# A fused attention and mixer kernel: chunk 3's first channel product in seven half-size products, the last stores in smaller pieces, and all jobs in another order

## The chip, the core and the metric

The kernel runs on one NeuronCore of a Trainium2 chip. The core has TensorE (PE, matmuls; PEld is its loading of weights), VectorE (DVE), ScalarE (ACT), GpSimd (POOL) and SyncE (SP). Each engine works through its own list of instructions in order and waits on semaphores for the others. PE writes only to the eight banks of PSUM, which VectorE and ScalarE read; DMAs move data between HBM and on-chip memory and are issued by SP, ACT and POOL. The metric is the time of one execution on the device in microseconds.

## The reference, cut to what matters

```python
q_p, k_p = phi(q * scale), phi(k * scale)     # exp features, 128 of them; batch 8, heads 8, seq 576, dim 64
kv  = einsum('bhsm,bhsd->bhmd', k_p, v);  z = sum(k_p, axis=2)
x   = einsum('bhsm,bhmd->bhsd', q_p, kv) / (einsum('bhsm,bhm->bhs', q_p, z) + 1e-6)
x   = x.transpose(0, 2, 1, 3).reshape(8, 576, 512)
h   = relu(x^T @ w_tok1) @ w_tok2             # token mixing: 576 -> 256 -> 576
u   = x + h^T
out = u + relu(u @ w_ch1) @ w_ch2             # channel mixing: 512 -> 1536 -> 512
```

Inputs and output are float32; the matmuls run on float16 operands.

## The kernel before

The work is cut into nine chunks of 512 rows for the channel mixing: chunk b (0 to 7) is the first 512 rows of batch b, and chunk 8 holds the 64 remaining rows of all eight batches. For each batch there are three stages.

*Attention* (`attention`): `kp` and `qp` are the feature matmuls (L702, L714) and `kt`, `qt` those of the 64 last rows (L594, L664); ScalarE takes their exponentials from the banks (L557); VectorE finds maxima (L735) and reciprocals; `vs_` scales v by them (L751, through the helper at L338); `kv` and `num` are the remaining products (L758, L791); `scale` divides the result out of the bank into x, on VectorE in one instruction (L809) or on ScalarE in five (L807).

*Token mixing* (`token_mix`): two products (L826, L839), an add that makes u (L842), and a DMA transpose on SP that turns u into uT (`ut_dma`, L847). For batches 2 to 7 q and k are cast by GpSimd's DMAs into a scratch in HBM and come back through DMA transposes on SP into qT and kT (`back`, L423); each of the two has three buffers.

*Channel mixing* (`channel_mix`): the second product, r3 @ w_ch2, uses seven half-size products instead of eight (`channel_out_fast`, L984, 256 columns each) in chunks 1 to 8; VectorE or GpSimd makes the half-sums S (L928), and VectorE reads the banks and adds (`read`, L964). The first product, uT @ w_ch1, has two forms. The plain one takes twelve blocks of four matmuls of 512 columns (L1167; L1173 and L1175 for chunk 0's first two) and a relu for each block. The fast one (`channel_in_fast`, chunks from `FAST_IN` on) takes three groups of seven products of four matmuls of 256 columns (L1096). Per group ScalarE copies three partial banks out (`keep`, L1115), VectorE joins them with later banks (`join`, L1120), and relus follow. Its operands are four differences of uT per chunk (L1067) and, once for all chunks, eight differences of w_ch1 (`weight_sums`, L1052), which occupy one buffer each of qT and kT from then on.

The order of the work is written out. Every piece of work is a job with a number, given in the order in which the functions add them. `ORDER` lists all job numbers in the order in which they are put into the engines' lists; a negative number is a filler matmul on zeros (`warm`, L1241). `SLOT` gives the buffer number of each tile, `MOVED` the engine of a job where it isn't the usual one. The planner only checks this order; it chooses nothing. A dependence becomes a semaphore wait, so a job early in `ORDER` can still wait. Jobs marked `port=True` on VectorE and GpSimd also wait for each other in turn (`turns`), so that they do not run at the same time.

The stores of chunks 2 to 7 are two per chunk (L1026), those of chunk 8 twelve (L1019).

Job numbers that the prediction's steps use (new numbers where they differ): 0 is the identity; 7, 17, 12 and 10 are loads (k's tail, w_tok1, the two halves of q); 1219 is chunk 7's kT transpose, 960 chunk 5's uT transpose; 1132, 1134 and 1130 are the last of chunk 6's second token products, 1023, 1025, 1027 and 1030 four output products of chunk 5, 859 and 860 stores of chunk 4, 1396 a tail transpose, 1138 chunk 6's uT transpose, 1175 chunk 6's first channel product.

Of the kernel before, what the change touches and what calls it, by code (L numbers as in the profile page):

```python
# [208 lines left out]
def kernel(  # L209
# [12 lines left out]
    nc = tc.nc  # L222
# [3 lines left out]
    DM = H * D  # L226
# [8 lines left out]
    NCB = DC // P  # L235
    NU = H // 2
    R = SM // 2
    RT = ST // 2
    RA = R + RT
    NPE = 2  # L240
    FAST_IN = 4
    SPLIT = ()
    HALVES = ()
    RW = S * 4 // P
    c_scale = float(1.0 / math.sqrt(math.sqrt(D)))

    pool = ctx.enter_context(tc.tile_pool(name="sb", bufs=1))
# [1027 lines left out]
```

## Time and profile before

| | us |
|---|---|
| runs | 272.42, 274.98, 272.96 |
| median | 272.96 |
| span of the profiled execution (its total is not given beside it) | 271.2 |
| TensorE busy | 262.6 |
| VectorE busy | 225.1 |
| ScalarE busy | 167.4 |
| GpSimd busy | 149.9 |

The span runs from the first to the last instruction of one profiled execution; the times of the runs also hold what lies around it. An engine's busy time is the union of its instructions. The granted TensorE clock is 0.997 of full speed over the span. A row of the chain of waits has a start, a length and what ran; a row of the waits has the waiting engine and line, what it waited for, the total, how often, and the longest; a row of the timeline has a start, a length, engine, line, operation, out<-in, shapes and count, and in brackets the idle time before it.

### The profile page before, as it was taken

Reading aid. Unit: us, or ns where it says so; the run is one execution under the profiler, and the core shown is the slowest. Engines: PE = TensorE matmul, PEld = TensorE weight load, DVE = VectorE, ACT = ScalarE, POOL = GpSimd, SP = SyncE. Lnnn points to the kernel's source line nnn. Section 1 sums busy time; section 2 is a strip of 40 time slices with the busy share of each in tenths; the row PEclk is TensorE's granted clock in tenths of the full one; section 3 lists DMA queues with packets and bytes.
Section 4 is the critical chain, followed back from the end, with each engine's and each line's share of the span. In section 5 each row is a group of like instructions: output and inputs, shape, how many; then the busy total and the mean of one; then the engine's idle time right before and its main releaser. Section 6 shows DMA issues by size and latency. Waiting matters only on the chain.

```text
span 271.2 us, 6792 instructions
## 1 busy us (share of the span) xinstructions
PE 262.6 (97%) x2683; PEld 183.9 (68%) x2683; DVE 225.1 (83%) x483; ACT 167.4 (62%) x395; POOL 149.9 (55%) x155
## 2 busy tenths in 40 slices
PE   8899999999999999999999999999999999999992
PEld 4457455444557655775468687886698688888882
DVE  3888879759879779988888989989987986899882
ACT  2999942179683639637965989777768342482400
POOL 8895393066882694662898893692551025404041
PEclk9999999999999999999999999999999999999998
DMA  7999999998999999999846999701160182030026
GB/s 195 191 208 210 191 211 183 192 217 148 196 234 172 251 219 150 163 236 192 163 91 103 214 130 221 187 2 77 39 139 2 21 155 81 2 155 2 19 87 209
DMA packets 81297, 39.72 MB, mean 146 GB/s; under 512 B 63984, under 2 KB 77040, under 8 KB 81072
## 3 DMA queue, kind: packets, MB, share of 16 engines
q0 software_dynamic: 31744, 17.74, 44.1%
q1 hardware_dynamic: 46928, 15.37, 28.5%
q10 hardware_dynamic: 2592, 6.16, 6.0%
q8 instruction: 21, 0.34, 0.5%
q14 instruction: 12, 0.10, 0.1%
HBM read 35.95 MB, written 16.52 MB: 193 GB/s over the span
## 4 chain that ended last, share of the span: by engine, by line
PE 91%; ACT 3%; DMA 3%; DVE 1%; issue 0%
PE bank L984 27%; PE bank L1096 16%; PE bank L1167 15%; PE bank L826 5%; PE bank L839 5%; PE bank L1201 4%; PE bank L791 3%; PE bank L702 3%; PE bank L758 3%; DMA kT<-k 3%; PE bank L714 2%; PE bank L1241 1%; ACT kp L557 1%; PE bank L513 1%; PE bank L793 1%; PE bank L819 1%
## 5 line engine op out<-in xcount | busy, mean ns | idle before, releaser
L338 POOL TENSOR_TENSOR vs<-v,vs 128x512 f16<-128x512 f16 x31 | 32.7, 1060 | 24.4 <-DVE vs L739 9.6
L1167 PE MATMUL bank<-uT,wc 128*128 128x512 f16 x184 | 44.1, 379 | 0.0
L557 ACT ACTIVATE kp<-bank 128x512 f16<-128x512 f32 x64 | 34.9, 617 | 14.5 <-PE bank L702 14.5
L333 ACT ACTIVATE r<-bank 128x512 f16<-128x512 f32 (+1 forms) x52 | 30.6, 607 | 19.4 <-PE bank L1167 8.4
L984 PEld LDWEIGHTS <-r 128*128 128x128 f16 x384 | 36.6, 98 | 6.5 <-issue 1.9
L735 DVE TENSOR_REDUCE km<-kp 128x8 f16<-128x1024 f16 x32 | 38.2, 1203 | 2.3 <-ACT kp L557 2.3
L557 ACT ACTIVATE qp<-bank 128x512 f16<-128x512 f32 x64 | 35.6, 620 | 3.4 <-PE bank L714 3.4
L338 POOL TENSOR_TENSOR r<-r 128x768 f16<-128x768 f16 x9 | 14.7, 1641 | 33.7 <-DVE S L338 20.5
L984 PEld LDWEIGHTS <-S 128*128 128x128 f16 x288 | 27.7, 98 | 4.0 <-DVE S L338 0.3
L1167 PEld LDWEIGHTS <-wc 128*128 128x128 f16 x184 | 16.4, 97 | 16.7 <-issue 1.0
L984 PE MATMUL bank<-T,r 128*128 128x256 f16 x192 | 23.6, 273 | 0.0
L984 PE MATMUL bank<-T,S 128*128 128x256 f16 x192 | 23.6, 273 | 0.0
L984 PE MATMUL bank<-wc,r 128*128 128x256 f16 x192 | 23.3, 273 | 0.0
L807 ACT ACTIVATE x<-bank,rc 128x64 f16<-128x64 f32 x90 | 20.6, 353 | 4.3 <-DVE rc L798 2.9
L338 POOL TENSOR_TENSOR S<-r,S 128x768 f16<-128x768 f16 x10 | 16.3, 1644 | 11.8 <-DVE r L338 9.3
L809 DVE TENSOR_TENSOR x<-bank,rc 128x320 f16<-128x320 f32 x46 | 21.5, 482 | 0.8
L335 DVE TENSOR_SCALAR r<-bank 128x512 f16<-128x512 f32 (+1 forms) x29 | 19.0, 664 | 3.6 <-PE bank L1167 2.4
L964 DVE TENSOR_TENSOR o<-u,bank 128x512 f32<-128x512 f16 x28 | 18.9, 676 | 3.5 <-PE bank L984 3.4
L1096 PE MATMUL bank<-uT,wc 128*128 128x256 f16 x156 | 21.1, 273 | 0.0
L842 DVE TENSOR_TENSOR u<-x,bank 128x512 f16<-128x512 f16 x28 | 17.9, 682 | 2.2 <-PE bank L839 2.0
L1096 PEld LDWEIGHTS <-wc 128*128 128x128 f16 x180 | 17.1, 98 | 2.7
L791 PEld LDWEIGHTS <-qp 128*128 128x128 f16 x256 | 13.6, 98 | 4.2 <-issue 0.4
(157 smaller groups left out, 576.0 us busy)
## 6 DMA issues: line engine op xcount, KB each, us to landing
out_dram<-o ACTq DMA_DIRECT2D x9, 512.0 KB, 3.1
q<-in_q_dram POOLq DMA_DIRECT2D x6, 576.0 KB, 7.9
wc<-in_moe_w_ch_dram POOLq DMA_DIRECT2D x4, 768.0 KB, 10.6
k<-in_k_dram POOLq DMA_DIRECT2D x6, 512.0 KB, 8.1
v<-in_v_dram POOLq DMA_DIRECT2D x6, 512.0 KB, 8.0
out_dram<-o SPq DMA_DIRECT2D x5, 512.0 KB, 3.4
r<-in_q_dram POOLq DMA_DIRECT2D x4, 288.0 KB, 7.2
v<-in_v_dram POOLq DMA_DIRECT2D x4, 256.0 KB, 8.9
```

The source lines that it names most:

```text
L333: nc.scalar.activation(out=out, in_=in_, func=AF.Relu)
L335: nc.vector.tensor_relu(out=out, in_=in_)
L338: (nc.gpsimd if eng == "POOL" else nc.vector).tensor_tensor(**kw)
L557: nc.scalar.activation(out=out, in_=in_, func=AF.Exp, bias=0.0, scale=1.0)
L735: nc.vector.reduce_max(out=t_km[place("km", (b, hp))], in_=src_, axis=AX.X)
L791: nc.tensor.matmul(ps[:, k, j * 65 : (j + 1) * 65], st, s[:, i, 0 : D + 1], start=True, stop=True)
L807: nc.scalar.activation(out=to[:, j], in_=ps[:, j], func=AF.Copy, scale=rc[:, j : j + 1])
L809: nc.vector.tensor_tensor(out=to, in0=ps, in1=rc.unsqueeze(2).broadcast_to((P, NJ + 1, D)), op=ALU.mult)
L964: nc.vector.tensor_tensor(out=o, in0=a, in1=ps, op=ALU.add)
L984: nc.tensor.matmul(ps[:, j * DH : (j + 1) * DH], a[:, cb, j * P : (j + 1) * P], w[:, cb, :], start=(bank_of(b, j0) not in held and j == j0 ...
L1096: nc.tensor.matmul(ps[:, n, :], w(a)[:, (2 * m + n) * P : (2 * m + n + 1) * P], x_[:, a], start=(what in ("P1", "P2", "P5") and n == 0 and ...
L1167: nc.tensor.matmul(ps, wc1[:, db, cb * P : (cb + 1) * P], moving(db), start=(db == 0), stop=(db == ND - 1))
```

## The change

`FAST_IN` goes from 4 to 3, so that chunk 3's first channel product takes the fast form as chunks 4 to 8 do, and `weight_sums` is placed before chunk 3. The tail's store of the block "22" is cut into two pieces and leaves from SP and ACT by default; chunk 7's second store is cut into its right and its left half. The job numbers shift accordingly (1500 jobs for 1469), and `ORDER`, `SLOT` and `MOVED` are new throughout, with 15 fillers instead of 16. `MOVED` puts, among others, 24 evictions of x on ScalarE instead of 18, 20 products `vs_` on GpSimd instead of 31, 30 half-sums S on GpSimd instead of 24, 20 differences of uT there instead of 11, and 10 of the copies `keep` on VectorE instead of none.

```diff
 ORDER = [
-    2, 5, 0, 6, 3, 1, 4, 16, 14, 18, 15, 7, 38, 12, -1, -2, -3, -4, -5, 39, 40, -6, 45, 9, 8, 47, 46, 10, 112, 41,
...
+    7, 2, 16, 5, 17, 12, 10, 0, 9, 1, 38, -8, -7, 39, 40, 14, 49, 50, 18, 45, 6, 3, 47, 48, 46, 112, 69, 114, 113,
+    70, 72, 71, 4, 41, 43, 21, 11, 8, 13, 29, 28, 19, 22, 30, 20, 73, 42, 118, 44, 129, 54, 78, 95, 130, 79, 80, 96,
...
+    1117, 1084, 818, 834, 1118, 1219, 684, 960, 961, 1223, 1233, 1077, 1225, 1224, 1235, 1079, 1234, 1078, 832, 819,
...
+    1272, 1271, 1132, 1133, 1134, 1130, 1135, 1131, 1023, 1236, 1253, 1287, 1025, 1255, 1254, 1276, 1264, 1288,
+    1238, 1289, 1237, 1277, 859, 860, 1396, 1138, 1017, 1016, 1020, 1024, 1290, 1027, 1261, 1247, 1278, 1281, 1244,
+    1265, 1291, 1026, 1292, 1293, 1028, 1030, 1245, 1294, 1248, 1246, 1282, 1283, 1266, 1279, 1295, 1296, 1297,
+    1249, 1280, 1175, 1298, 1144, 1143, 1262, 1031, 1299, 1178, 1300, 1139, 1140, 1263, 1022, 1018, 1142, 1159,
...
+    1465, 1466, 1469, 1388, 1463, 1467, 1455, 1475, 1471, 1472, 1476, 1477, 1470, 1391, 1453, 1457, 1486, 1487,
+    1490, 1491, 1473, 1474, 1482, 1483, 1478, 1479, 1496, 1497, 1492, 1493, 1480, 1481, 1494, 1495, 1488, 1489,
+    1484, 1485, 1499, 1498,
 ]
...
-    FAST_IN = 4
+    FAST_IN = 3
...
-            for i, js, cols, need in ((0, (0, 2), left, "11"), (1, (0, 2), right, "22"), (0, (0, 1), right, "12"), (0, (1, 2), right, "12"),
-                                      (1, (0, 1), left, "21"), (1, (1, 2), left, "21")):
+            for i, js, cols, need in ((0, (0, 2), left, "11"), (1, (0, 1), right, "22"), (1, (1, 2), right, "22"), (0, (0, 1), right, "12"),
+                                      (0, (1, 2), right, "12"), (1, (0, 1), left, "21"), (1, (1, 2), left, "21")):
                 for h in range(2):
-                    eng = engine("POOL" if need == "22" else "ACT" if h else "SP")
+                    eng = engine("ACT" if h else "SP")
...
-        for i, need in ((0, ["11", "12"]), (1, ["21", "22"])):
+        pieces = [(0, slice(0, DM), ["11", "12"])]
+        if c < B - 1:
+            pieces.append((1, slice(0, DM), ["21", "22"]))
+        else:
+            pieces += [(1, slice(DH, DM), ["22"]), (1, slice(0, DH), ["21"])]
+        for i, cols, need in pieces:
             eng = engine("SP")
-            def store(i=i, eng=eng):
-                (nc.scalar if eng == "ACT" else nc.sync).dma_start(out=out[c, 0:SM, :].rearrange("(p j) d -> p j d", j=NJ)[:, 2 * i : 2 * i + 2, :], in_=o_of(i))
+            def store(i=i, cols=cols, eng=eng):
+                (nc.scalar if eng == "ACT" else nc.sync).dma_start(
+                    out=out[c, 0:SM, :].rearrange("(p j) d -> p j d", j=NJ)[:, 2 * i : 2 * i + 2, cols], in_=o_of(i)[:, :, cols])
             dma(eng, key + 0.9 + 0.1 * i, 1.3, store, deps=[outs[x, 0] for x in need], give=[o_tag(i)], cost=0.4)
```

In the new `ORDER`, the numbers on SP's queue around the places that the prediction names are, in this order: 784 (chunk 4's uT), 1219, 684 (a store of chunk 3), 960, and later 859, 860, 1396, 1138. Before it was 1110 for chunk 6's uT, 932 for chunk 5's, and chunk 7's kT was 1191, behind 932. Between chunk 6's second token products and its first channel product PE has, in the new list, 1023, three `qp`, 1025, a `kv`, a `num`, 1027, five `num`, a `kv`, 1030 and a `num`.

More of the change, by code (lines that the diff above doesn't have):

```diff
@@ L22 @@
 ORDER = [
[72 rows of a table removed]
[73 rows of a table added]
 ]
 SLOT = (
-    "0100234050600701103402521706330411560210401223120233033711614250603121274011353162700434056100673712"
-    "5604012137412011364072310230050171020343162253332400316147113252670150234273510456726122307162037060"
-    "2101403611743101500672132341016022340210153710060304721221311256200137405034166217310045360007231160"
-    "0514120035104163352201116013521130226023322300247231215031762225103506445703673205406111010711533212"
-    "1607431356207050146101037210023042621132416151237110114621370004437262522017230341625300127411073652"
@@ L102 @@
-    "7052306430302500224170306211134520211603340201152261201003530146001042170476635123150410171020302341"
-    "0713007123003024072311231042171200363451106172341125001274320451011005735620031131500035146134011672"
-    "3350140201372623547000632172523461301322524114020721020456357476031036732361103062040230607211045210"
-    "713221066004351206702201016412202076415102"
+    "0010203450670010102315407026132510700231246110175023271340351163304522012017423030455673071061570423"
+    "1643520117216004523311271460110123002761502413361072101356711420222150234003750614567371004020301743"
@@ new lines @@
+    "1120036105427650322110042230176051013110012170635325311406230271412040173551347266025313741001602013"
+    "7425110074335217420100112213122514701023041507131013642174233424067705425361570600302416011500720311"
+    "1611024173300203610422030721213046121032110331423673305010627120124103671431455121301027502230220331"
+    "0003365610213400710500224336711024030761103400120470633200111274060502763074150226047533012625701103"
+    "1021231314267415326014235210614332140511106314701530231067514111107504333162550012016202200151677567"
@@ L106 @@
+    "1034103022000216235174320362500123417120021135421137143507712502060074312630125423350630421075136012"
+    "0134021030232613475013200017103625600123167400"
 )
 MOVED = {
-    44: "ACT", 48: "ACT", 53: "ACT", 61: "ACT", 64: "ACT", 67: "ACT", 68: "ACT", 108: "ACT", 120: "DVE",
-    122: "ACT", 128: "ACT", 139: "ACT", 147: "DVE", 149: "DVE", 153: "DVE", 157: "ACT", 159: "DVE", 167: "DVE",
-    171: "DVE", 173: "DVE", 175: "ACT", 179: "DVE", 185: "DVE", 191: "ACT", 197: "ACT", 207: "ACT", 208: "DVE",
@@ L111 @@
-    229: "ACT", 246: "ACT", 304: "DVE", 314: "DVE", 316: "DVE", 320: "DVE", 322: "DVE", 328: "POOL", 334: "POOL",
-    350: "ACT", 402: "ACT", 413: "DVE", 436: "ACT", 439: "DVE", 452: "DVE", 454: "DVE", 456: "DVE", 458: "DVE",
-    468: "DVE", 470: "DVE", 478: "POOL", 482: "POOL", 527: "DVE", 550: "ACT", 561: "DVE", 564: "ACT", 602: "DVE",
-    604: "DVE", 606: "DVE", 624: "DVE", 627: "POOL", 628: "POOL", 629: "POOL", 630: "POOL", 631: "POOL",
-    632: "POOL", 647: "ACT", 648: "ACT", 711: "DVE", 717: "ACT", 734: "ACT", 739: "DVE", 750: "POOL", 751: "POOL",
@@ L116 @@
-    752: "POOL", 753: "POOL", 756: "POOL", 757: "POOL", 758: "POOL", 760: "POOL", 809: "POOL", 810: "POOL",
-    812: "POOL", 814: "POOL", 816: "POOL", 831: "ACT", 861: "DVE", 878: "DVE", 898: "ACT", 901: "ACT",
-    936: "POOL", 937: "POOL", 938: "POOL", 952: "DVE", 953: "ACT", 954: "ACT", 970: "ACT", 987: "POOL",
-    988: "POOL", 992: "POOL", 1009: "ACT", 1039: "DVE", 1045: "ACT", 1059: "ACT", 1076: "ACT", 1093: "ACT",
-    1099: "DVE", 1101: "DVE", 1113: "POOL", 1145: "ACT", 1146: "ACT", 1162: "ACT", 1164: "POOL", 1168: "POOL",
@@ L121 @@
-    1185: "ACT", 1186: "ACT", 1235: "ACT", 1238: "ACT", 1252: "ACT", 1255: "ACT", 1289: "POOL", 1292: "POOL",
-    1324: "ACT", 1338: "DVE", 1342: "POOL", 1348: "POOL", 1363: "ACT", 1364: "ACT", 1371: "POOL", 1372: "POOL",
-    1404: "ACT", 1419: "ACT", 1420: "ACT", 1424: "POOL", 1428: "POOL",
+    42: "DVE", 44: "ACT", 46: "ACT", 50: "DVE", 52: "ACT", 58: "ACT", 59: "ACT", 61: "ACT", 67: "ACT", 86: "DVE",
+    103: "DVE", 108: "ACT", 120: "DVE", 137: "DVE", 139: "ACT", 147: "DVE", 149: "DVE", 157: "ACT", 161: "ACT",
@@ new lines @@
+    164: "DVE", 173: "DVE", 183: "ACT", 185: "DVE", 187: "DVE", 191: "ACT", 202: "ACT", 206: "ACT", 208: "DVE",
+    227: "DVE", 266: "ACT", 278: "DVE", 289: "DVE", 304: "DVE", 314: "DVE", 318: "DVE", 326: "DVE", 328: "POOL",
+    330: "POOL", 332: "POOL", 334: "POOL", 350: "ACT", 377: "DVE", 394: "DVE", 396: "DVE", 402: "ACT", 411: "DVE",
+    413: "DVE", 419: "ACT", 428: "DVE", 433: "ACT", 439: "DVE", 456: "DVE", 458: "DVE", 466: "DVE", 476: "POOL",
+    477: "POOL", 478: "POOL", 481: "POOL", 482: "POOL", 527: "DVE", 533: "ACT", 542: "DVE", 547: "ACT", 559: "DVE",
@@ new lines @@
+    561: "DVE", 584: "ACT", 587: "DVE", 603: "POOL", 605: "POOL", 606: "POOL", 609: "POOL", 610: "POOL",
+    611: "POOL", 612: "POOL", 660: "ACT", 662: "POOL", 666: "POOL", 713: "DVE", 716: "ACT", 736: "ACT", 750: "ACT",
+    767: "ACT", 785: "POOL", 786: "POOL", 787: "POOL", 788: "POOL", 792: "DVE", 803: "ACT", 804: "ACT", 813: "DVE",
+    840: "POOL", 842: "POOL", 844: "POOL", 889: "DVE", 892: "ACT", 909: "ACT", 926: "ACT", 940: "DVE", 943: "ACT",
+    946: "ACT", 963: "POOL", 965: "POOL", 966: "POOL", 981: "ACT", 982: "ACT", 997: "ACT", 998: "ACT", 1013: "ACT",
@@ new lines @@
+    1014: "ACT", 1017: "POOL", 1019: "POOL", 1020: "POOL", 1022: "POOL", 1037: "ACT", 1067: "DVE", 1073: "ACT",
+    1087: "ACT", 1104: "ACT", 1107: "ACT", 1139: "POOL", 1141: "POOL", 1142: "POOL", 1146: "DVE", 1165: "DVE",
+    1174: "ACT", 1181: "DVE", 1189: "ACT", 1190: "ACT", 1192: "POOL", 1194: "POOL", 1196: "POOL", 1198: "POOL",
+    1213: "ACT", 1249: "ACT", 1260: "DVE", 1280: "ACT", 1300: "ACT", 1317: "POOL", 1319: "POOL", 1320: "POOL",
+    1324: "DVE", 1334: "DVE", 1335: "ACT", 1336: "ACT", 1345: "DVE", 1352: "ACT", 1367: "ACT", 1368: "ACT",
@@ L124 @@
+    1370: "POOL", 1372: "POOL", 1373: "POOL", 1374: "POOL", 1376: "POOL", 1391: "ACT", 1398: "POOL", 1399: "POOL",
+    1400: "POOL", 1405: "DVE", 1416: "ACT", 1426: "DVE", 1431: "DVE", 1432: "ACT", 1433: "ACT", 1440: "DVE",
+    1453: "POOL", 1455: "POOL", 1457: "POOL", 1486: "ACT", 1487: "SP", 1488: "POOL", 1489: "POOL", 1492: "ACT",
+    1493: "SP", 1494: "ACT", 1495: "SP",
 }
```

134 rows, old and new, of the table ORDER are left out of this document.

## Prediction

> **What bounds the kernel now.** I read the page first, then the waits of TensorE alone, then the chain of waits in order of time, and last the stretches.
>
> ```profile
> span 271.2 us, 6792 instructions
> PE 262.6 (97%) x2683; PEld 183.9 (68%) x2683; DVE 225.1 (83%) x483; ACT 167.4 (62%) x395; POOL 149.9 (55%) x155
> ...
> PE 91%; ACT 3%; DMA 3%; DVE 1%; issue 0%
> ```
> ```profile
> PE bank L1241 <- DVE S L1238: 1.2, 1, 1.2
> PE bank L702 <- ACT kT L329: 0.7, 2, 0.5
> PE bank L594 <- DMA kT<-k: 0.6, 1, 0.6
> PE bank L594 <- ACT kp L557: 0.3, 1, 0.3
> PE bank L865 <- DVE kT L329: 0.2, 1, 0.2
> ```
> TensorE is busy for 97% of the span, and 91% of the chain is TensorE. A busy TensorE can still be a slow one, so its waits count: they are 3.0 us in all, and only the 0.6 us at L594 lies behind the opening. What remains must be the rate of the matmuls, which the chain shows:
>
> ```profile
> 29.57 0.81 PE bank L1173 x3
> ...
> 92.12 5.18 PE bank L1167 x24
> ...
> 162.69 7.32 DMA kT<-k
> ...
> 170.06 0.28 PE bank L594 x4
> ...
> 235.24 8.73 PE bank L1096 x80
> ...
> 253.14 13.13 PE bank L984 x120
> 266.29 0.42 DVE x L964
> ```
> Twenty-four matmuls of 512 columns take 5.18 us, 216 ns each; eighty of 256 columns take 8.73 us, 109 ns each. From chunk 0's channel product at 29.57 until 266.3 TensorE runs at such rates. So the kernel is an opening of 29.6 us, 236.7 us of matmuls with 0.6 us of waiting, and an end of 4.9 us. Only matmul work, that wait, the opening and the end can make it shorter.
>
> **The change part by part.** *Chunk 3's product.* Removed: 12 blocks of 4 matmuls, 48 x 215.8 ns = 10.36 us. Added: 3 groups of 7 products of 4 matmuls of 256 columns, 84 x 109.1 ns = 9.17 us. TensorE: **-1.19 us**, all of it on the path.
>
> A rule speaks against this. The Trainium skill, "TensorE: Matmul & The Clock Gate", section "Back-to-back issue gap", gives about 131 ns a matmul at 512 columns and 81 ns at 128 in a sustained stream; between them I estimate 98 ns for 256, and then the old blocks would cost 6.3 us, the new ones 8.2 us, and the sum would be 1.9 us up instead of 1.19 down. The rows above, 216 and 109 ns, do not agree with it.
>
> What the other engines get for it (groups by line with shapes kept apart: busy us, mean ns of one, idle time before and who ended it):
>
> ```profile
> L338 POOL TENSOR_TENSOR vs<-v,vs 128x512 f16<-128x512 f16 x31 | 32.7, 1060 | 24.4 <-DVE vs L739 9.6 <-DVE r L335 6.3 <-PE bank L765 3.6
> ...
> L333 ACT ACTIVATE r<-bank 128x512 f16<-128x512 f32 x50 | 29.7, 613 | 19.4 <-PE bank L1167 8.4 <-PE bank L826 8.0 <-PE bank L1096 3.0
> ...
> L809 DVE TENSOR_TENSOR x<-bank,rc 128x320 f16<-128x320 f32 x46 | 21.5, 482 | 0.8
> ...
> L335 DVE TENSOR_SCALAR r<-bank 128x512 f16<-128x512 f32 x27 | 18.2, 682 | 3.1 <-PE bank L1167 2.4 <-PE bank L826 0.6
> L842 DVE TENSOR_TENSOR u<-x,bank 128x512 f16<-128x512 f16 x28 | 17.9, 682 | 2.2 <-PE bank L839 2.0
> ...
> L1120 DVE TENSOR_TENSOR r<-kp,bank 128x512 f16<-128x512 f32 x15 | 10.2, 682 | 1.3 <-issue 0.4 <-PE bank L1096 0.4 <-ACT kp L329 0.4
> ...
> L329 ACT COPY kp<-bank 128x512 f32<-128x512 f32 x15 | 8.9, 600 | 6.4 <-PE bank L1096 6.2 <-ACT kvsb L329 0.2
> ...
> L338 DVE TENSOR_TENSOR S<-r 128x768 f16<-128x768 f16 x13 | 6.9, 554 | 1.4 <-issue 0.5 <-ACT r L333 0.4 <-POOL S L338 0.2
> ...
> L338 POOL TENSOR_TENSOR uT<-uT,uT 128x512 f16<-128x512 f16 x5 | 5.8, 1158 | 1.4 <-DVE S L338 1.4
> ...
> L335 DVE TENSOR_SCALAR r<-r 128x1024 f16<-128x1024 f16 x12 | 4.8, 422 | 0.2
> ...
> L333 ACT ACTIVATE r<-r 128x512 f16<-128x512 f16 x7 | 4.4, 630 | 4.5 <-DVE r L1120 4.5
> ...
> L335 DVE TENSOR_SCALAR r<-r 128x512 f16<-128x512 f16 x8 | 2.3, 288 | 0.1
> ...
> L338 DVE TENSOR_TENSOR vs<-v,vs 128x512 f16<-128x512 f16 x1 | 0.6, 641 | 0.0
> ```
> The engine of each job is its usual one unless the table MOVED names another. VectorE gains 9 joins (9 x 0.682), 3 relus of 1024 columns (3 x 0.422) and 2 of 512 (2 x 0.288), gets 4 more of this chunk's half-sums (4 x 0.554), and loses 4 relus from the banks (4 x 0.682): +7.5 us. ScalarE gains 9 copies (0.600), 3 relus (0.613) and one of 0.630, and loses 8 relus (0.613): +3.0 us. GpSimd gains the 4 differences of uT (1.158 each). The eight weight sums only move a chunk earlier. Whether this hides is read from the stretch:
>
> ```profile
> 120.00:151.00 31.00, 31.00 (x359) 20.23 (x357) 26.10 (x60) 22.46 (x58) 22.56 (x22) 1.00 0.82 154
> 151.00:170.00 19.00, 18.48 (x197) 13.36 (x193) 17.90 (x40) 16.94 (x41) 14.39 (x13) 1.00 1.10 190
> ```
> (Columns: length, busy PE, its weight loads, DVE, ACT, POOL, granted clock, DMA, GB/s.) Chunk 3's stage has 31 us with 26.1 of VectorE. Its own +7.5 would make 33.6 us and overrun the 29.8 us that TensorE then has. But MOVED also shifts other jobs: in the new list, between the first channel products of chunks 3 and 4, VectorE keeps 6 attention evictions (0.482) instead of 9, and ScalarE gets 8 instead of 3. Added up by such rows, VectorE has 31.0 us there and had 30.1 (26.1 in the stretch, as neighbours overlap), so I take 26.9 us of 29.8, or 90%; in the next stretch it ran at 94% (17.90 of 19.00) with TensorE hardly waiting. By the same scaling (30.3 by rows, 26.2 before, 22.46 in the stretch) ScalarE gets 26.0, 87%. Cost: 0; bounds 0 to +3.8 (33.6 - 29.8).
>
> *The wait at L594.* The transpose into kT took 7.32 us and came 0.6 us late. In the new list chunk 7's kT transpose stands on SyncE's queue ahead of chunk 5's uT transpose, not behind it, so it can leave some 15 us earlier. **-0.6 us**, bounds -0.6 and 0.
>
> *New order elsewhere.* A wait can open in its place:
>
> ```profile
> L847 SPq DMA_TRANSPOSE uT<-u x7: 1760/2787/3427, 53.9 to 218.9; - x7
> ...
> DMA to landing us min/median/max: 4.3/5.2/6.0
> ```
> The tightest place that I find is chunk 6. Between its last token product and its first channel product the new list has four full output products (12 x 0.109 = 1.31 us each) and about 2.2 us of attention: 7.4 us, where the old list had 9.1. In it must fit one or two adds (L842, 0.68 each) and the transpose, 4.3 to 6.0 us: 5.0 to 7.4. On SyncE it also stands behind two stores of chunk 4 and one tail transpose, whose data are ready by then. It just fits; I take 0, bounds 0 to +1.3 (a transpose as slow as the one of 7.32).
>
> *Opening.*
>
> ```profile
> 1.02 0.29 POOL masks.py:199 TENSOR_SCALAR_AFFINE_SELECT S<-S 128x128 f32<-128x128 f32 x1
> 2.72 0.63 POOL L373 DMA_DIRECT2D r<-in_k_dram  x1
> 3.84 2.13 PE L513 MATMUL bank<-S,wc 128*128 128x128 f32 x8
> 6.55 1.08 ACT L557 ACTIVATE kp<-bank 128x512 f16<-128x512 f32 x2 [3.49 <-PE bank L702]
> 18.68 1.28 ACT L807 ACTIVATE x<-bank,rc 128x64 f16<-128x64 f32 x5
> ```
> GpSimd now issues four loads before it makes the identity that the first transposes need: 4 x about 0.6 us, so it is ready near 3.6 instead of 1.3, and the transposes start near 4.4 instead of 3.84, with ScalarE's first exp behind them: +0.6. Against it, one of chunk 0's evictions goes from ScalarE (1.28) to VectorE (0.482), and its three products on GpSimd go to VectorE. Fifteen filler matmuls replace sixteen; they run in waits. Sum 0, bounds -1.6 and +2.6 (both below).
>
> *End.*
>
> ```profile
> L1019 ACTq DMA_DIRECT2D out_dram<-x x5: 520/603/726, 262.2 to 267.0; - x5
> ...
> DMA to landing us min/median/max: 2.0/3.1/6.0
> ```
> VectorE's last read ends at 266.7, and ScalarE issues its last store only at 267.0, behind another. Chunk 7's left and right halves and a half of the tail's "22" block leave earlier now. After the last read one store on each of SyncE and ScalarE remains, as before. I take **-0.2 us**; bounds -1.1 (a landing of 2.0 for 3.1) and +0.6 (one more issue ahead).
>
> Sum: -1.19 - 0.6 - 0.2 = -2.0 on the profiled 271.2, so a span of 269.2. The median of the runs, 272.96, stands 1.8 above that span; with the same 1.8 I predict **271.0 us**.
>
> **The rivals.** *Shorter opening, too.* If chunk 0 hangs on VectorE's chain, the eviction saves 0.8 and two of the moved products (1060 ns on GpSimd, 641 on VectorE) save 0.4 each: 1.6 us, **269.4**. For it: the loads start earlier. Against it: the later identity. Chance 0.29.
>
> *VectorE becomes the bound* (slower than before). Place: chunk 3's stage. It decides once more than 29.8 us of VectorE work must be done there, so if the 3 evictions and the other moved jobs do not leave it when it matters. Price up to 3.8 us: **274.8**. For it: 94% in the next stretch, which now begins with VectorE already behind. Against it: the new counts, 90%. Chance 0.12.
>
> *Opening later.* The first token weights (524 KB) and q now go out among the k loads. At the opening's rate that is 524 KB / 198 GB/s = 2.6 us:
>
> ```profile
> 0.00:20.00 20.00, 17.15 (x233) 9.79 (x234) 13.34 (x37) 14.62 (x37) 17.73 (x29) 1.00 1.06 198
> ```
> That gives **273.6** if the k loads wait for all of it. The Trainium skill, "DMA: Bandwidth & Descriptors", section "Issuing engines are not separate DMA queues", says that transfers of all issuing engines run on the same 16 DMA engines and interleave, which is this mechanism; no run here shows it yet. Against it: ScalarE has other work queued meanwhile. Chance 0.08.
>
> *The saving does not come*, because 256-column matmuls pay for their weight loads when mixed with attention: 271.0 + 1.2 = 272.2. The row of eighty speaks against it. Chance 0.05. The page's 131 ns, as a mechanism of this kernel (512 columns faster than 2 x 256), gives 274.1: 0.01.
>
> **How the numbers follow.** The forecast has 0.45. A measurement of this kernel tells about 1% (2.7 us) from no change: 270.2 and 275.7. Below 270.2 lie the shorter opening and a little of the forecast's own spread: 0.31. Above 275.7 lies only VectorE's bound together with a late opening or a late transpose (274.8 + 1.3 or more): 0.10. The rest, 0.59, is within 1%. The range from 268.6 (shorter opening and the end's best case) to 274.8 leaves out 0.2.
>
> **What would show it.** TensorE: 84 more matmuls of 256 columns on the fast product's line, at 109 ns; 48 fewer of 512; no wait of L594 for kT. VectorE's share in chunk 3's stage near 90%. Chunk 0's first channel product near 29.6. From the last matmul to the span's end 4.7 us. I am wrong if that first product moves by over 1 us, if TensorE shows waits behind the opening of over 1 us in sum, or if VectorE is on the chain in chunk 3.

## The result: 7% slower

The changed kernel takes 292.96 us (median; 291.85 to 299.97), the kernel before, on the same chip, 272.98. The ratio is 1.0714, with a 95% interval of 1.066 to 1.0767. I had predicted 271.0 us, between 268.6 and 274.8. The profiled execution of the changed kernel took 293.41 us with a span of 291.6, against 271.2 before: 20.4 us to be found. Single executions of kernels in which the mechanism found below is at work lie up to 28 us apart, for a reason that no run shows, so I read those from the profiled execution, and give its span beside the median where it matters.

### The profile page after: what moved, and what is told of

Read it like the earlier page. It is cut to its first block, busy times and chain, and to the rows that moved or that the text cites. A ratio compares the mean times of both kernels' runs of the same rounds, so it can differ in the third digit from the quotient of the medians.

```text
span 291.6 us, 6909 instructions
## 1 busy us (share of the span) xinstructions
PE 265.2 (91%) x2718; PEld 190.2 (65%) x2718; DVE 231.6 (79%) x487; ACT 182.8 (63%) x432; POOL 154.8 (53%) x157
## 4 chain that ended last, share of the span: by engine, by line
PE 71%; DMA 16%; DVE 6%; POOL 4%; issue 1%; ACT 1%; POOLq 0%; DVEq 0%
PE bank L990 25%; PE bank L1108 16%; DMA kT<-k 8%; PE bank L1179 6%; DMA uT<-u 4%; PE bank L845 3%; PE bank L832 3%; PE bank L1213 3%; DVE km L741 3%; PE bank L797 2%; PE bank L708 2%; DMA k<-in_k_dram 2%; PE bank L764 2%; DMA r<-in_k_dram 2%; DVE vs L344 2%; PE bank L720 1%
## 5 line engine op out<-in xcount | busy, mean ns | idle before, releaser
L344 POOL TENSOR_TENSOR r<-r 128x768 f16<-128x768 f16 x12 | 19.5, 1639 | 26.7 <-DVE S L344 25.1
L1179 PE MATMUL bank<-uT,wc 128*128 128x512 f16 x136 | 32.4, 379 | 0.0
L1108 PE MATMUL bank<-uT,wc 128*128 128x256 f16 x192 | 28.2, 279 | 3.9 <-DMA uT<-u 3.9
L344 POOL TENSOR_TENSOR vs<-v,vs 128x512 f16<-128x512 f16 x20 | 21.0, 1057 | 15.8 <-DVE vs L745 12.5
L344 POOL TENSOR_TENSOR S<-r,S 128x768 f16<-128x768 f16 x13 | 21.2, 1637 | 14.4 <-DVE vbd L645 11.7
L813 ACT ACTIVATE x<-bank,rc 128x64 f16<-128x64 f32 x120 | 26.9, 348 | 2.8 <-DVE rc L804 2.5
L344 POOL TENSOR_TENSOR uT<-uT 128x512 f16<-128x512 f16 x10 | 11.5, 1151 | 31.1 <-DMA uT<-u 20.7
L990 PE MATMUL bank<-wc,r 128*128 128x256 f16 x192 | 26.0, 291 | 0.0
L1108 PEld LDWEIGHTS <-wc 128*128 128x128 f16 x216 | 20.5, 99 | 8.0 <-DMA uT<-u 4.6
L1108 PE MATMUL bank<-uT,qT 128*128 128x256 f16 x108 | 19.2, 273 | 0.0
L1108 PE MATMUL bank<-uT,kT 128*128 128x256 f16 x108 | 18.9, 273 | 0.0
```

What stands on the lines that cost most here:

```text
L344: (nc.gpsimd if eng == "POOL" else nc.vector).tensor_tensor(**kw)
L813: nc.scalar.activation(out=to[:, j], in_=ps[:, j], func=AF.Copy, scale=rc[:, j : j + 1])
L990: nc.tensor.matmul(ps[:, j * DH : (j + 1) * DH], a[:, cb, j * P : (j + 1) * P], w[:, cb, :], start=(bank_of(b, j0) not in held and j == j0 ...
L1108: nc.tensor.matmul(ps[:, n, :], w(a)[:, (2 * m + n) * P : (2 * m + n + 1) * P], x_[:, a], start=(what in ("P1", "P2", "P5") and n == 0 and ...
L1179: nc.tensor.matmul(ps, wc1[:, db, cb * P : (cb + 1) * P], moving(db), start=(db == 0), stop=(db == ND - 1))
```

## The profile after

The changed kernel's page, then its waits of TensorE (us in total, times, longest):

```profile
span 291.6 us, 6909 instructions
...
PE 265.2 (91%) x2718; PEld 190.2 (65%) x2718; DVE 231.6 (79%) x487; ACT 182.8 (63%) x432; POOL 154.8 (53%) x157
...
PEclk9999999999995599999999999779999999999999
...
PE 71%; DMA 16%; DVE 6%; POOL 4%; issue 1%; ACT 1%; POOLq 0%; DVEq 0%
```
```profile
PE bank L600 <- DMA kT<-k: 11.6, 2, 10.7
PE bank L1108 <- DMA uT<-u: 3.9, 1, 3.9
```
TensorE falls from 97% to 91%, and transfers take 16% of the chain where they took 3%. Two places stand out: a stop of 10.7 us for kT at L600 (L594 before) and one of 3.9 us for uT at L1108 (L1096 before). The first two slices of a low granted clock, 5 and 5 tenths, span the long stop and the work right behind it (87 to 102 us). The chain in order of time shows the same places:

```profile
1.29 5.36 DMA r<-in_k_dram
...
30.67 0.75 PE bank L1185 x3
...
73.54 22.13 DMA kT<-k
...
96.96 2.67 PE bank L990 x12
...
176.75 11.74 DMA uT<-u
...
287.68 0.42 DVE x L970
```
Chunk 3's kT transpose takes 22.1 us; the slowest of the kernel before took 7.3. Chunk 5's uT takes 11.7, where seven took 4.3 to 6.0. Behind the long stop twelve matmuls of 256 columns take 2.67 us instead of 1.31.

The sum by stage: the first channel product comes at 30.67 instead of 29.57 (+1.1). From there to VectorE's last read it is 257.0 us instead of 236.7 (+20.3). From that read to the span's end it is 4.0 instead of 4.9 (-0.9). Of the 20.3, waits for transposes are 11.6 + 3.9 - 0.6 = 14.9; some 4 more are the half clock behind them, 2.2 behind the long stop and 2.1 behind the other, by the distances between the starts of matmuls of one shape (213 ns instead of 109 at 256 columns). What is left, about 1 us, I did not follow to its end.

Why is the transpose slow? SyncE's queue in the changed kernel, then in the one before, at chunk 3's transposes (start, time to issue):

```profile
67.65 5.09 SPq L429 DMA_TRANSPOSE qT<-q  x1
72.84 0.53 SPq L1223 DMA_DIRECT2D out_dram<-o  x1
73.54 14.66 SPq L429 DMA_TRANSPOSE kT<-k  x1
```
```profile
66.45 2.88 SPq L423 DMA_TRANSPOSE qT<-q  x1
69.50 2.54 SPq L423 DMA_TRANSPOSE kT<-k  x1
```
The transpose starts 4.0 us later than before (73.54 for 69.50), behind a qT whose issue takes 5.09 us instead of 2.88 and behind a store; the other 15 us of its delay are its own length. And GpSimd, which issues the loads, over the same time in the changed kernel and before:

```profile
62.05 0.54 POOL L408 DMA_DIRECT2D q<-in_q_dram  x1
62.58 0.57 POOL L413 DMA_DIRECT2D k<-in_k_dram  x1
63.14 1.25 POOL L400 DMA_DIRECT2D vt<-in_v_dram  x2
64.37 3.30 POOL L419 DMA_DIRECT2D k<-in_k_dram  x4
69.23 1.05 POOL L344 TENSOR_TENSOR vbd<-vt,vbd 128x512 f16<-128x512 f16 x1 [1.56 <-DVE vbd L645]
70.23 0.97 POOL L386 DMA_DIRECT2D v<-in_v_dram  x1
71.19 1.09 POOL L413 DMA_DIRECT2D k<-in_k_dram  x2
...
73.41 0.93 POOL L386 DMA_DIRECT2D v<-in_v_dram  x1
74.31 0.66 POOL L400 DMA_DIRECT2D vt<-in_v_dram  x1
```
```profile
68.99 1.06 POOL L338 TENSOR_TENSOR vs<-v,vs 128x512 f16<-128x512 f16 x1 [1.39 <-PE bank L765]
70.01 1.64 POOL L338 TENSOR_TENSOR qT<-wc 128x768 f16<-128x768 f16 x1
71.59 1.69 POOL L413 DMA_DIRECT2D k<-in_k_dram  x2
```
Before, four products vs, a vbd and a weight sum of GpSimd stood between chunk 3's loads and the next ones, so nothing more was issued until 71.6, when both transposes were nearly issued. In the new list the four products are VectorE's and the loads stand elsewhere in the order (no run moves the products alone): six small loads leave at once behind chunk 3's, and seven more, five of them of 512 or 576 KB, from 70.2 on, across the issue of kT. My theory (A) is that these loads, ahead of the transpose and beside it, hold it up. The rivals are that the transpose has another cause in the new list (B), or that the new list and the seven products cost time of their own (C).

## Experiments

### The loads into the old kernel

In the kernel before, the four jobs of six small loads go behind the third vs or vbd, and the seven others behind the weight sum 753:

```diff
-    395, 411, 368, 749,
+    395, 411, 504, 505, 650, 834, 368, 749,
...
-    424, 753, 401,
+    424, 753, 506, 651, 835, 649, 654, 656, 655, 401,
```


> The kernel before, with nothing changed but the order of GpSimd's loads: the tail loads of chunks 3, 4 and 5 ahead of the transposes of chunk 3, and six loads of chunks 3 to 5 together behind them, as the changed kernel has them. Theory A: chunk 3's kT transpose takes over 14 us instead of 7.2, TensorE waits 5 to 12 us for it at L594, and the time is 280 to 288. Theory B: the transposes hold their place, TensorE waits below 1 us for them, and the time stays within 1.5 us of the kernel before.

Measured: 286.33 us median, 279.8 to 288.74; profiled span 287.0. Its only large wait of TensorE, and the chain (this file's lines are 26 lower):

```profile
PE bank L568 <- DMA kT<-k: 12.4, 1, 12.4
```
```profile
69.42 23.04 DMA kT<-k
```
Theory A stands: with no product, no store and no engine changed, the load order alone gives the changed kernel's stop, 13 us in the median and 7 in the mildest of four executions. The two halves by themselves:

```diff
-    395, 411, 368, 749,
+    395, 411, 504, 505, 650, 834, 368, 749,
```


> The kernel before with only the six small loads (32 KB each) of the run loads_ahead put ahead of chunk 3's transposes; the large loads keep their places. If the small loads ahead of a transpose hold it up, its issue takes over 6 us, it lands 5 to 15 us later than in the kernel before, and the time is 276 to 286. If the large loads beside it do, the time stays within 1.5 us of the kernel before.

```diff
-    424, 753, 401,
+    424, 753, 506, 651, 835, 649, 654, 656, 655, 401,
```


> The kernel before with only the seven loads that run loads_ahead put in one batch behind chunk 3's transposes (five of 512 or 576 KB). If loads issued just behind a transpose take its bandwidth, chunk 3's kT lands 5 us or more later and the time is 276 to 286. If a transpose that is issued before them keeps its place, TensorE waits below 2 us for it, and the time stays within 2 us of the kernel before.

Measured: 289.97 (276.96 to 298.1; profiled span 275.2) for the six small ones, 281.11 (ratio 1.0278, 1.0241 to 1.0315) for the seven. The transposes' issues and landings, small loads first:

```profile
kT<-k SPq DMA_TRANSPOSE x1, 12.3
```
```profile
qT<-q SPq DMA_TRANSPOSE x1, 8.9
kT<-k SPq DMA_TRANSPOSE x1, 8.7
```
Six loads of 32 KB ahead cost the transpose 5 us even in the mildest execution. The seven behind it cost it 1.5 us (8.7 for 7.2), as one that is issued first mostly keeps its place; my either-or was too plain. But they cost 8 us of time in a way that I had not thought of (GpSimd, VectorE and TensorE of that run):

```profile
79.77 0.85 POOL L413 DMA_DIRECT2D k<-in_k_dram  x1 [2.92 <-DMA v<-in_v_dram]
...
82.90 1.65 POOL L338 TENSOR_TENSOR r<-r 128x768 f16<-128x768 f16 x1
```
```profile
84.58 0.56 DVE L338 TENSOR_TENSOR r<-r 128x768 f16<-128x768 f16 x1 [7.45 <-POOL r L338]
```
```profile
PE bank L984 <- DVE o L964: 5.4, 1, 5.4
```
With eight loads on their way GpSimd's ninth waits for the first to land (so it does in loads_behind, for 6.85 us), and a half-sum behind it on the queue waits too; VectorE waits 7.45 us for that and TensorE 5.4 for VectorE.

### The loads out of the changed kernel's way

```diff
-    501, 502, 504, 505, 686, 862, 365, 506, 687, 863, 685, 690, 692, 691, 311,
+    501, 502, 365, 506, 504, 505, 686, 687, 685, 690, 692, 691, 311,
...
-    332, 328, 334, 868,
+    332, 328, 334, 862, 863, 868,
```


> The changed kernel with seven of GpSimd's loads put later on its queue: the tail loads of v for chunk 3 and of k for chunk 4 behind chunk 3's main load of v, and chunk 5's two k loads behind the half-sums of chunk 1. Nothing else differs. Theory A (chunk 3's kT transpose took 22.1 us because some fifteen loads were queued ahead of it and beside it): chunk 3's kT lands below 80 us, TensorE's wait of 10.7 us at L600 falls below 2 us, the half clock behind it goes too, and the time falls by 11 to 14 us, to 279 to 282. Theory B (the transpose is late for another reason, VectorE's added work or its place behind a store on SyncE's queue): the wait stays above 8 us and the time stays above 289.

Measured: 302.28 median, 287.76 to 316.18. In the mildest, profiled execution (span 286.0) chunk 3's kT was issued from 71.27 to 79.42, beside the load batch that now began at 70.4, and took 16.6 us; TensorE's longest wait for kT fell from 10.7 to 3.4. The median is higher than the changed kernel's and the mildest execution lower, but neither is near 279 to 282, so the expectation failed: the batch still ran across the issue. To be rid of that, the batch was made to wait for the transpose:

```diff
-    439, 503, 197,
+    439, 503, 506, 504, 505, 686, 687, 685, 690, 692, 691, 197,
...
             job.fn()
+            made = list(nc.cur_bb.bb.instructions[n:])
+            if job is self.jobs[503]:
+                self.gate = made[-1].name
+            if job is self.jobs[506]:
+                tc.add_manual_dep(made[0], self.gate, after, reason="gate")
```


> The changed kernel with nine of GpSimd's loads (v, q and k of chunks 3 and 4) made to wait until chunk 3's kT transpose has landed, and chunk 5's two k loads behind the half-sums of chunk 1. Theory A (the transpose is slow while loads are issued ahead of it and beside it): chunk 3's kT is issued in 2.5 to 3.5 us, lands below 78 us, and the stop of 11 us at that place is gone; what is left over the kernel before comes from the same collision at later transposes. Theory B (the slow transpose has a cause of its own in the new order): it still takes over 12 us from issue to landing.

Measured: 293.33 median, 285.17 to 294.2. Its kT at that place, and SyncE's queue:

```profile
kT<-k SPq DMA_TRANSPOSE x1, 6.3
```
```profile
70.19 2.29 SPq L434 DMA_TRANSPOSE kT<-k  x1
...
87.47 31.16 SPq L434 DMA_TRANSPOSE kT<-k  x2
```
Theory B is out: alone, the same transpose on the same queue lands in 6.3 us, and the stop at that place is gone. The next two kT, now among the delayed loads, are issued only by 118.6, 31 us after the first of them began. The collision was moved, not removed. TensorE waits 1.9 us for kT and 4.0 for uT there, but also 4.7 for VectorE and 5.0 for GpSimd, so what is left over the kernel before is only in part the same collision.

Chunk 3's kT, from issue to landing, in one profiled execution of each, in order of its length:

| run | kT, us |
|---|---|
| gate (nothing beside it) | 6.3 |
| before | 7.2 |
| mains_together | 8.7 |
| tails_ahead | 12.3 |
| loads_behind | 16.6 |
| changed | 22.1 |
| loads_ahead | 23.0 |

So loads of GpSimd's queue slow a transpose of SyncE's. The changed kernel's trace also shows how they share the engines. Its queues from 82 to 86 us (q0 is GpSimd's, q1 SyncE's; packets, MB, share of the engines):

```profile
q0 software_dynamic: 134, 0.92, 110.4%
q1 hardware_dynamic: 134, 0.03, 6.1%
```
The numbers of packets are the same, and nearly so in the two stretches of 4 us that follow: 767 and 775, 1086 and 1083. A load's packet carries some 6.9 KB from 82 to 86 us and the transpose's 0.2, so the transpose moves 0.03 MB beside 0.92. Not every stretch is so even: in loads_ahead, from 84 to 88 us, it is 141 against 67. Small loads are small in bytes alone: in tails_ahead, from 70 to 74 us, GpSimd's queue has 2196 packets for 0.08 MB, and SyncE's moves 0.43 MB, where the kernel before moves 0.72 with no packet of GpSimd's.

The Trainium skill, "DMA: Bandwidth & Descriptors", section "Queues, rings and completion order", says that each DMA engine takes turns between the queues that have work, a packet at a time. The equal numbers of packets from 82 to 94 us agree with it; whether its packet and the profile's are the same unit is not shown.

### The second place, and the old blocks

The run loads_behind, with chunk 7's kT put behind chunk 5's uT as well:

```diff
-    1118, 1219, 684, 960, 961,
+    1118, 684, 960, 1219, 961,
```


> The run before, and chunk 7's kT transpose put behind chunk 5's uT transpose on SyncE's queue. Theory A (the same cause twice: the uT transpose took 11.7 us because the kT transpose and two loads were in the queue ahead of it): uT takes below 8 us, TensorE's wait of 3.9 us at L1108 falls below 1 us, and the time falls by 4 to 6 us more, to 274 to 277. Rival (kT of chunk 7 is then late in its place, as in the kernel before, or the wait for uT comes from its own late inputs): less than 2 us is gained.

Measured: 302.85 median (297.08 to 308.2). In the profiled execution the wait for uT fell to 0.4 us, and a wait of about 3 us for chunk 7's kT took its place, as the rival said; a stop of 15.5 us for an earlier kT hid all else.

That kernel with the blocks again:

```diff
-    FAST_IN = 3
+    FAST_IN = 4
```


> The run before with chunk 3's first channel product in 12 blocks of four matmuls of 512 columns again, at the same places of the order; its sums, copies and joins are left out. The step of the prediction (the seven products save 1.19 us of TensorE and VectorE's 7.5 us hide): 1.2 us slower than the run before. Rival (VectorE's work does not hide): 1 to 4 us faster than the run before.

Measured: 301.28 (293.74 to 319.93). The scatter is larger than the effect; nothing follows.

### The product into the old list, the end alone, and two lists joined

```diff
-    FAST_IN = 4
+    FAST_IN = 3
```


> The kernel before with chunk 3's first channel product by seven half-size products and nothing else: its order stays, the new sums, products, copies and joins are put in where the twelve blocks stood, two attention evictions of chunk 4 go to ScalarE, and the slots follow. The step of the prediction: 1.2 us faster than the kernel before (271.6 to 272.2), with VectorE's work hidden. Rival (VectorE becomes the bound in that stage): 1 to 4 us slower, with TensorE waiting for VectorE's joins or evictions between 120 and 155 us.

Measured: 283.31; ratio 1.0365 (1.0323 to 1.0407). TensorE's waits are short ones for the product's copies and joins and for evictions, 1.7 us at most, spread from 112 to 142 us (one more, of 1.8 us for a kT, comes later). The chain there goes through ScalarE and VectorE: the product, put in by hand, is bound by its own sequence. That a searched list hides it is seen below; in a list made for blocks it costs 10 us.

```diff
-            for i, js, cols, need in ((0, (0, 2), left, "11"), (1, (0, 2), right, "22"), (0, (0, 1), right, "12"), (0, (1, 2), right, "12"),
+            for i, js, cols, need in ((0, (0, 2), left, "11"), (1, (0, 1), right, "22"), (1, (1, 2), right, "22"), (0, (0, 1), right, "12"),
```


> The kernel before with the last stores in smaller pieces, as the changed kernel has them, and from the last 38 entries of the list on in the changed kernel's order; nothing else. The step of the prediction: 0.2 us faster, between 1.1 faster and 0.6 slower. What the changed kernel's own profile suggests (4.0 us from the last matmul to the end instead of 4.9): 0.9 us faster, 272.2 to 272.4.

Measured: 272.49, ratio 0.9983 (0.9962 to 1.0004), span 270.5: 0.7 us less, about what the profile said, and not told from no change.

```diff
-    479, 480, 660, 684, 656, 1188, 704,
+    479, 480, 696, 720, 692, 606, 862, 863, 691, 868, 608, 604, 1041, 481, 477, 722,
...
-    921, 1217, 641,
+    921, 1217, 1215, 1044, 1045, 1046, 1216, 641,
```


> The kernel before's list up to entry 607 (chunk 4's transposes are issued), then the changed kernel's list for all that is left, with chunk 3's seven products and the small last stores in it; of that rest the loads of chunks 6 and 7 are put some places earlier on GpSimd's queue. If the parts are worth what the prediction and the profile give them (product -0.7 to -1.2 us, end -0.9) and only the collisions made the changed kernel slow: 270.5 to 271.8. If the product's work does not hide, or the new list is slow in itself: above 274, with waits of TensorE for VectorE in chunk 3's stage.

```diff
-    921, 1217, 1215, 1044, 1045, 1046, 1216, 641,
+    921, 1217, 641,
...
-    662, 666, 1221, 1222, 938,
+    662, 666, 1044, 938, 1216, 1045, 1046,
```


> The run crossed with the loads of chunks 6 and 7 at the changed kernel's places. If they hold up the transposes there: TensorE waits 3 us or more for chunk 5's uT or chunk 7's kT and it is 3 to 7 us slower than crossed. If not: the same within 1 us.

```diff
-    692, 606, 862, 863, 691, 868, 608, 604, 1041, 481, 477,
+    692, 691, 481, 477,
...
-    861, 549,
+    861, 862, 863, 549,
...
-    482, 478, 703,
+    482, 478, 868, 1041, 703,
...
-    762, 611, 609, 610,
+    762, 606, 611, 609, 610, 608, 604,
```


> The run crossed with its seam mended, where TensorE waited 14 us in sum for work that the joining of the two lists had put late: chunk 5's k loads leave ahead of chunk 6's q load, v of chunk 5 and k of chunk 6 behind chunk 2's half-sums, three half-sums of chunk 2 are VectorE's again, and the last three weight sums stand just ahead of chunk 3's uT sums. If only the seam was slow in crossed and the changed list's rest is sound once its loads keep clear of the transposes: 270.5 to 272. If the rest is slow too: above 275 with waits behind 125 us.

Measured: 290.43 (1.0627, 1.0595 to 1.0658), 292.77 (1.0676, 1.0617 to 1.0735) and 284.56 (1.0426, 1.0409 to 1.0444). All three missed: at the seam (80 to 130 us) TensorE stopped for 14, 12 and 6 us in sum, for a kT behind its late load and for half-sums behind weight sums. Behind the seam they say what they were made for; in crossed TensorE waits only 1.0 us in sum there. Chunk 5's uT with the loads of chunks 6 and 7 at the changed kernel's place, and with them earlier:

```profile
177.72 11.98 DMA uT<-u
```
```profile
uT<-u SPq DMA_TRANSPOSE x1, 4.3
```
The wait of 3.9 us for uT is there in the one and gone in the other: the changed kernel's second stop is the same collision. The whole difference, 2.3 us, is below the 3 to 7 expected, and within the spread of crossed_raw's executions (290.05 to 295.59).

### The loads all but taken away

A row instead of a chunk is copied for q and k of chunks 3 to 7, and their transposes read chunk 2's copy. The lists stay as they are.

```diff
             def cast(w=w):
+                if b > 2:
+                    nc.gpsimd.dma_start(out=scratch[w, b][0:1, 0:D], in_=src[w][b, 0, 0:1, :])
+                    return
...
-                nc.sync.dma_start_transpose(out=t.unsqueeze(1), in_=scratch[w, b])
+                nc.sync.dma_start_transpose(out=t.unsqueeze(1), in_=scratch[w, 2])
```


> The kernel before, with part of the work left out: the copies of q and k of chunks 3 to 7 on GpSimd's queue carry one row of 64 numbers each instead of a whole chunk, and the transposes of chunks 3 to 7 read chunk 2's copy. The list of instructions, their engines and the transposes stay. Control: its only wait behind the opening is 0.6 us, so both theories expect 271 to 273.5.

> The changed kernel with the same copies of q and k left out. Theory A (the loss is the collision of loads with transposes): the waits for kT and uT fall below 2 us in sum and the time falls from 293 to 271 to 275, within 2 us of the control. Theory C (the new list is slow in itself, by waits that the collisions only show): it stays above 280.

Measured: 273.09 for the old list, 273.45 for the new one; against the kernel before 1.0001 (0.9982 to 1.002) and 1.0006 (0.9977 to 1.0034). All waits of TensorE in the new list that are left (its lines here are 10 higher):

```profile
PE bank L511 <- DVE S L509: 2.5, 1, 2.5
PE bank L563 <- DMA r<-in_k_dram: 1.7, 1, 1.7
PE bank L1263 <- DVE S L1260: 1.2, 1, 1.2
PE bank L774 <- DVE vs L344: 1.2, 2, 0.8
```
The old list does not care for these loads; the new one loses its 20 us with them, and no wait for kT or uT is left. Theory C falls: with these loads gone, list and products cost nothing that the medians show. What the run does not part is how: a transpose here no longer queues behind copies, and no longer waits for its own either.

The last two tell the rest. First the blocks again, in the new list without those loads; then, with the products, one step of the opening moved:

```diff
-    FAST_IN = 3
+    FAST_IN = 4
```


> The run after_few_loads with chunk 3's first channel product in twelve blocks of four matmuls of 512 columns again. The step of the prediction (the products save 1.19 us and VectorE's work hides): 0.7 to 1.2 us slower than after_few_loads. If VectorE's added work costs: faster by 1 to 4 us. If neither tells: within 0.5 us.

```diff
-    39, 40, 14, 49, 50, 18, 45, 6, 3, 47, 48, 46,
+    39, 40, 14, 18, 45, 6, 3, 47, 49, 48, 50, 46,
```


> The run after_few_loads with one step of the opening moved: the four transposes of k's tail (L553 of the changed kernel), which wait for a load that lands at 6.65 us, stand behind the first eight transposes of k (L519) on TensorE's queue instead of ahead of them. If that wait sets the opening, the eight transposes start near 4.9 us instead of 7.0 and chunk 0's first channel product comes 0.5 to 1.5 us earlier. If VectorE's or GpSimd's chain behind it sets the opening, the product stays within 0.3 us.

Measured: 278.52 for the blocks, 5.1 slower than after_few_loads and more than expected. Its waits between 112 and 150 us add up to 3 us and more (1.5 at a token matmul, 0.8 for vs): again a stage put in by hand. By the medians of the distances between starts, 216 and 109 ns, the matmuls alone are 1.2 us longer. And 272.65 for the opening (0.9985 of the kernel before, 0.9971 to 0.9998), 0.8 less than after_few_loads in the median and 1.6 in the profiled span (270.7 for 272.3). TensorE's first steps there:

```profile
4.70 0.29 PE L511 MATMUL bank<-ident,S 128*128 128x128 f16 x1 [2.47 <-DVE S L509]
4.80 1.94 PE L529 MATMUL bank<-S,wc 128*128 128x128 f32 x8
```
The eight transposes start at 4.80; in the changed kernel it was 7.01, behind the tail's:

```profile
6.69 0.39 PE L553 MATMUL bank<-ident,r 64*128 64x64 f16 x4 [1.71 <-DMA r<-in_k_dram]
7.01 1.97 PE L519 MATMUL bank<-S,wc 128*128 128x128 f32 x8
```
The first channel product, without the step and with it:

```profile
31.05 0.75 PE bank L1195 x3
```
```profile
29.52 0.75 PE bank L1195 x3
```
It moves by 1.5 us. That wait sets the opening.

## Why the prediction was wrong, point by point

- **New order elsewhere: cost 0, bounds 0 to +1.3. This step failed.** I looked for a transpose with too little cover, and took its length as given, from 4.3 to 7.3 us. The list also sets when loads leave, and with them around it the same transpose took 22.1. loads_ahead shows that the load order is enough, gate that without it the transpose is as short as before, after_few_loads that with the loads gone so is the loss. I had counted that vs products leave GpSimd, for VectorE's sum; I did not ask what moves up on GpSimd's queue when they do.
- **The wait at L594: -0.6.** This failed too. Chunk 7's kT left 14 us earlier, as I had it (11.2 us ahead of chunk 5's uT instead of 3.0 behind), but I put that down as a gain alone. It took 18.4 us instead of 7.3 there, and uT behind it 11.7: 3.9 us of wait for uT and 0.9 for the same kT in place of 0.6.

```profile
kT<-k SPq DMA_TRANSPOSE x1, 18.4
```
  crossed and crossed_raw show that the loads of chunks 6 and 7 do it.
- **Chunk 3's product: -1.19, hidden.** Right in mechanism. Without those loads the matmuls differ by 1.2 us at the median distances, and in the changed kernel's stage TensorE never waits:

```profile
138.14:167.60 29.46, 29.46 (x364) 23.05 (x360) 28.10 (x69) 28.54 (x83) 16.62 (x17) 1.00 0.84 136
```
  VectorE is at 95% and ScalarE at 97%, where I had 90 and 87: the cover is thinner than my sum, and it is the list's; by hand it opened (product_alone, blocks_few_loads). Sixteen matmuls of 512 columns take 3.45 us in the changed kernel's chain and twelve of 256 take 1.31, 216 and 109 ns each. The 131 ns of the Trainium skill, "TensorE: Matmul & The Clock Gate", section "Back-to-back issue gap", that spoke against the change are not borne out.
- **Opening: 0.** It cost 1.1 us. The identity's delay that I priced at 0.6 came, as 1.0 (4.80 for 3.84), and cost nothing by itself: with the step of the opening moved the first product comes at 29.52, and at 29.57 in the kernel before. That four transposes of k's tail stand ahead of the others and wait for a load until 6.69 I did not see. The rival "opening later" had the direction, but another cause and a price of 2.6.
- **End: -0.2.** It was -0.9, inside the bounds; -0.7 when alone.
- **The rivals.** VectorE did not become the bound. I named loads that interleave with other transfers, and priced them for the opening alone; in the middle they were the case itself, at some eight times that price. None of my rivals was slower than 274.8, so 0.10 for slower by over 1% was far too little.
- **The sum of what I did price** does not come even with the loads out of the way: the new list took 273.45 against 273.09, where product and end alone would make -1.4. The profiled spans, 272.3 and 271.3, differ by +1.2 in the opening, -0.7 at the end, and +0.4 between, where the product's -1.2 meets 1.2 us of waits for vs on VectorE; the other 0.4 is not explained. There was no gain of 2 us to have.

## What to carry to other kernels

A new order of instructions is also a new order of transfers. For each transfer that something waits for, list what is queued ahead of it and beside it on every queue, in packets as well as in bytes, and ask what held those loads back until now. Here it was their place in the order, behind compute on the issuing engine's queue. A transfer's duration from a profile holds only for the traffic that it was measured in.

## What the hardware showed that I had not expected

- A transpose of one chunk's kT took between 6.3 and 23.0 us, by the loads around it. Its issue on SyncE took from 2.3 (gate) to 14.7 us (the changed kernel; 7.7 in loads_ahead, where the landing was the latest), so all that is queued behind it leaves late as well.
- Six loads of only 32 KB ahead of a transpose cost it 5 us, and while large loads ran beside it the transpose got one packet of some 0.2 KB for each of theirs of 6.9 KB (134 and 134 in the changed kernel, from 82 to 86 us).
- The ninth load on GpSimd's queue waits for the first to land, and takes GpSimd's other work with it: 5.4 us of TensorE in mains_together. Whether the chip or the program sets the number eight is not shown.
- A stop costs more than its length, here 2.2 us more. In the changed kernel, per stretch (length, PE, its loads, DVE, ACT, POOL, granted clock, DMA, GB/s):

```profile
95.00:100.00 5.00, 4.29 (x42) 3.03 (x44) 1.39 (x4) 2.72 (x6) 1.52 (x1) 0.50 1.35 280
100.00:105.00 5.00, 5.00 (x51) 3.66 (x48) 4.33 (x8) 3.27 (x7) 3.03 (x5) 0.93 1.07 82
```
  The granted clock is 0.50 behind the stop of 10.7 us, and matmuls of 256 columns start 109 ns apart again only 5.0 us after work resumed at 95.7; behind the stop of 3.9 us for uT it is half for 4 us as well. The Trainium skill, "TensorE: Matmul & The Clock Gate", section "What's actually happening", has the clock at half after an idle window of about 3.4 us and back after as much sustained work. The trace agrees on the half clock; the way back took longer here.
